# Fetching one half of the transposed tiles between the stores of the other, and holding one batch's channel steps out of four of every six slots

## The chip, the cores and the metric

The kernel runs on one core of a Trainium2 chip. The metric is the device time of one execution in microseconds (us); lower is better. Besides it there is one profiled execution of the kernel before, with a trace of every instruction on the five engines and of the DMA packets.

## The reference

The program is a block-sparse attention followed by a Fourier mixer with a two-layer channel network, for 4 batches, 8 heads, 768 rows and head size 64 (512 columns when the heads stand side by side).

```python
# attention, per batch and head
scores = scale * q @ k.T                      # 768 x 768
scores = where(mask, scores, -1e9)            # mask of 32 x 32 blocks: window, first, last, sampled
attn   = exp(scores - max) / sum
x      = attn @ v                             # heads side by side: (768, 512) per batch
# mixer, per batch
mixed = real(fft(fft(x, axis=rows), axis=columns))
u     = x + mixed
un    = (u - mean(u)) / sqrt(var(u) + 1e-6)   # along the 512 columns
out   = u + relu(un @ w_ch1) @ w_ch2          # 512 -> 2048 -> 512
```

## The kernel before

**Slots.** Attention works on pairs of heads: 4 pairs for a batch, 16 in all. A pair is cut into 6 *slots* of two units each (128 keys by 384 queries, two heads), so there are 96 slots, numbered 0 to 95, and 24 of them make a *phase*, one for each batch. In `slot(sl)`, `phase, r = divmod(sl, SB)` gives the phase and the slot within it (0 to 23), and `n, s = divmod(sl, SP)` the pair and the slot within the *pair* (0 to 5). A slot does scores on TensorE (line 579), the exponential on ScalarE (607), the multiplication by the mask on VectorE (609, from the second batch's end on; before that TensorE adds the mask itself, line 589), the sums along the keys on GpSimd (639, or on VectorE in line 634) and the product with v on TensorE (653). Scores have two PSUM buffers, so a unit's scores wait until the mask multiplication two units earlier has read its buffer.

**The mixer of a batch** runs during the phase of the next batch, in two lists. `apart` holds the small steps, most of them VectorE work: folds, the two Fourier products, mean and variance (`spread`), whitening (`whiten`, kind "w", it waits for GpSimd's 1/sqrt, `rstd_at`), and then for each of two halves of three tiles `un_blocks`: VectorE transposes the whitened tile in 32 x 32 blocks and SyncE (SP) stores it to a scratch tensor in device memory (`far<-un`, line 1016, 256 KB). When all six are stored, `un_back` reads both halves back with the blocks in their transposed places, four DMAs of 192 KB for each half (`unT<-far`, line 1025, runs of 128 bytes). Four steps `right` of kind "b" (line 1057, VectorE) then need both halves. `late` holds the channel network: 4 rounds, each of two *quads* (line 1103, seven products in place of eight) and six *channel* steps (line 1268). If a round's first quad is started while attention stands still (`state["alone"]`), and it isn't the fourth, its second product is done with seven products in place of eight as well (`round_of`, line 1211, three steps in place of six).

**What sets the order.** The order of all instructions is fixed when the program is built, by a planner that keeps a clock of its own for every engine (`when`) and adds a cost written by hand for each step. Steps of `apart` go into gaps of TensorE (`gap`), and, in phases 2 and 3, up to four at the end of a slot while `late` is empty. A "b" step is taken only when the planner's clock has passed `state["back"]`, which `un_back` sets to its own time plus `BACK[b]`. Channel steps go into the odd slots by an allowance, `owed`: each slot adds `pace`, the planned time of `late` above `COVER` = 100 us divided by the slots left, between 2.5 and 9.6 us, and a step is taken while `owed` is at least half its cost (9.1 us a quad, 3.45 us a channel step; a whole batch is 155.6 us). In slot 4 of the first pair of phases 2 and 3, `until(..., s == 4)` takes all channel steps of the batch before last that are left, alone, until its first half is stored; the rest of the second half follows in the next slots.

**The SP queue** issues its DMAs in the order of the program: besides the two kinds above, the loads of q, k and v (`qb` line 231, `kb` line 231, `vr` line 271), the stores of the output (line 1279) and, for later pairs, the exchange of the attention's output through device memory, `row<-oT` (line 692) and `x<-row` (696). The tile `oT` has one buffer: VectorE's transpose into it (line 661) waits until the last `row<-oT` has read it.

Of the kernel before, what the change touches and what calls it, by code (L numbers as in the profile page):

```python
# [11 lines left out]
FP32 = mybir.dt.float32  # L12
# [10 lines left out]
def _words(ap, n):  # L23

    return bass.DRamTensorHandle(ap.tensor.name, (2 * n,), I32)
# [74 lines left out]
def kernel(  # L100
# [14 lines left out]
    nc = tc.nc  # L115
# [4 lines left out]
    P = 128  # L120
    C = S // P
    BLK = 32
# [5 lines left out]
    ND = DM // P  # L128
    NF = FF // P
    T = C // 2  # L130
# [51 lines left out]
    tr_p = ctx.enter_context(tc.tile_pool(name="tr_p", bufs=2))  # L182
# [11 lines left out]
    when = {"PE": 0.0, "ACT": 0.0, "DVE": 0.0, "POOL": 0.0}  # L194
    free = {"m": [0.0, 0.0], "t": [0.0]}

    def busy(engine, us, after=0.0):
        when[engine] = max(when[engine], after) + us
        return when[engine]
# [11 lines left out]
    HOP = 0.1  # L211
# [89 lines left out]
    def bit(n):  # L301
# [5 lines left out]
                      in_=bass.AP(tensor=_words(sampled_blocks, NB * NR), offset=0,  # L307
                                  ap=[[0, NB], [1, 2 * NB * NR]]))
# [183 lines left out]
    s_at, e_at, e_free, oT_at, acc_at = {}, {}, {}, {}, {}  # L492
# [100 lines left out]
    def weigh(u, s):  # L593
        n, w = divmod(u, UP)
        half, c = divmod(w, C)
        e = ep.tile([P, 2, HS], FP32, tag="e", name="e")
        e_of[u] = e
        if u in by_pe:
            nc.scalar.activation(out=e, in_=s[:, :, 0:HS], func=ACT.Exp, scale=scale)  # L599
            e_at[u] = busy("ACT", 0.8, max(s_at[u], e_free.pop(u - 2 * SLOT, 0.0))) + HOP  # L600
            if n >= NP:
                to_gather.append(u)

            if w >= UP - SLOT:
                gather_to(u)
        else:
            nc.scalar.activation(out=s[:, :, 0:HS], in_=s[:, :, 0:HS], func=ACT.Exp, scale=scale)  # L607
            m = mask[:, c, half * HS:(half + 1) * HS].rearrange("p (o s) -> p o s", o=1)
            nc.vector.tensor_tensor(out=e, in0=s[:, :, 0:HS], in1=m.broadcast_to([P, 2, HS]),  # L609
                                    op=ALU.mult)  # L610
            e_at[u] = busy("DVE", 0.97, busy("ACT", 0.8, s_at[u]) + HOP) + HOP
            gather_to(u)
            if n >= NP:
                gather(u)

    def gather_to(u):
        while to_gather and to_gather[0] <= u:
            gather(to_gather.popleft())

    def gather(u):  # L620


        n, w = divmod(u, UP)
        half, c = divmod(w, C)
        if c == 0:
            return
        if c == 1:
            acc_of[n, half] = acc_p.tile([P, 2, HS], FP32, tag="acc", name="acc")
        acc, e = acc_of[n, half], e_of[u]
        start = e_of[u - 1] if c == 1 else acc  # L630
        at = max(e_at[u], acc_at.get((n, half), 0.0))
        sooner = max(when["DVE"], at) + 1.0 < max(when["POOL"], at) + 2.9
        if u in by_pe and masks["by_pe"] and w < UP - SLOT and sooner:
            nc.vector.tensor_tensor(out=acc, in0=start, in1=e, op=ALU.add)
            acc_at[n, half] = busy("DVE", 1.0, at) + HOP
        else:

            for i in range(2):
                nc.gpsimd.tensor_add(out=acc[:, i, :], in0=start[:, i, :], in1=e[:, i, :])  # L639
            acc_at[n, half] = busy("POOL", 2.9, at) + HOP  # L640
        e_free[u] = acc_at[n, half]

    def values(u):
# [335 lines left out]
    rstd_at = deque()  # L979
# [3 lines left out]
    def mixer(b, xA, xB):  # L983


        uns, unT = {}, {}
# [21 lines left out]
        lines = {}  # L1008

        def un_blocks(half, m):  # L1010

            un = uns.pop((half, m))
            if half not in lines:
                lines[half] = far_p.tile([T, P, DM], FP32, tag=f"un{half}", name="far")
            nc.vector.transpose(out=un, in_=un)
            nc.sync.dma_start(out=lines[half][m], in_=un)

        def un_back():

            for half in range(2):  # L1020
                unT[half] = tr_p.tile([P, ND, T * P], FP32, tag="tr", name="unT")
                of = lines[half].rearrange("m (g j) (k a i) -> a j k (m g) i",
                                           j=BLK, a=P // BLK, i=BLK)
                for a in range(P // BLK):
                    nc.sync.dma_start(
                        out=unT[half][BLK * a:BLK * a + BLK].rearrange(
                            "j k (g i) -> j k g i", i=BLK),
                        in_=of[a])
            state["back"] = max(when["PE"], state["ready"]) + BACK[b]

        t, s = {}, {}
        K1, K2 = slice(0, ND // 2), slice(ND // 2, ND)
# [289 lines left out]
        def outputs(r, m, after):  # L1322
# [60 lines left out]
            if r == 1:  # L1383
# [5 lines left out]
              for h in range(2)]  # L1389

        ft = [[("d", lambda h=h, m=m: un_blocks(h, m), 0.0, 0.0, 0.7) for m in range(T)]
              for h in range(2)]

# [23 lines left out]
        for r in range(0 if last else NF // 4):  # L1417
# [9 lines left out]
    MOST, LEAST = 9.6, 2.5  # L1427
    COVER = 100.0
    AHEAD = 2.2
    BACK = 13.0, 12.0, 15.0  # L1430
    ALONE = 3.0
    LEAVES = 13.0
    SP = UP // SLOT
# [2 lines left out]
    short, apart, late, due = deque(), deque(), deque(), deque()  # L1436
    asked = set()
    needed = set()
    state = {"paired": False, "total": None, "w": 0, "got": 0, "owed": 0.0, "ready": 0.0,
             "back": 0.0, "place": None,  # L1440
             "alone": False, "drain": lambda: None}
# [10 lines left out]
    def do_apart():  # L1452
        kind, fn, pe, act, dve, _ = apart.popleft()
        if finished and kind[0] in "mt" and state["total"] in short:
            short.remove(state["total"])
            state["total"][2]()
        if kind[0] in "dwb":
            dve += behind(kind)
            state["ready"] = busy("DVE", dve, {"w": rstd_at[0] if rstd_at else 0.0,
                                               "b": state["back"]}.get(kind, state["ready"])) + HOP  # L1460
            fn()
            return
        done = state["ready"]
        if kind != "-":
            at = bank(kind[0])
            done = busy("PE", pe, done) + HOP
        fn()
        if act:
            done = busy("ACT", act, done) + HOP
        if dve:  # L1470
            done = busy("DVE", dve, done) + HOP
        if kind != "-":
            give(at, done - HOP)
        state["ready"] = done
# [44 lines left out]
    def begin(b):  # L1519


        before, after, rest = mixer(b, x_of[b, 0], x_of[b, 1])
        any_of = len(late) + len(apart) + 4 * len(rest)
        hold = 2 * T
        apart.extend((*step, any_of) for step in norm_steps(b) + before)
        apart.extend((*step, hold) for step in after)

        def go():
            late.extend(rest)
        apart.append(("-", go, 0.0, 0.0, 0.0, hold))  # L1530
# [21 lines left out]
    def slot(sl):  # L1552
        phase, r = divmod(sl, SB)
        n, s = divmod(sl, SP)
# [56 lines left out]
        if s >= ((4 if late else 5) if reuse else 3) and (n, 0) in oT_at and once(n):  # L1611
            b, j = pairs[n]
            at = oT_at[n, 0]
# [12 lines left out]
        if sl < B * SB and n % NP == 1 and s == 1:  # L1626
            b = pairs[n - 1][0]
            at = oT_at[n - 1, 1]
            if b >= 2:
                until(lambda: (b - 2, 1) in finished)  # L1630
                at = when["PE"] + LEAVES
# [22 lines left out]
        us = sum(step[1] for step in late)  # L1654
        pace = max(LEAST, min(MOST, (us - COVER) / left)) if left > 0 else MOST
        state["owed"] = min(state["owed"], pace) + pace if late else 0.0
        more = paired and opens and sl < B * SB
        if not more:
            gap(rest())
# [3 lines left out]
            gap(rest())  # L1663

        for _ in range(4 if phase > 1 and not late and len(apart) < 6 * T else 0):
            if apart and not late and (apart[0][0] != "b" or
                                       state["back"] < max(when["DVE"], when["PE"]) + 0.2):
                do_apart()


# [6 lines left out]
        while short and (not more or soon) and (  # L1677
                s in must or len(short) > 1 or phase == 0 or soon or sl == B * SB):
            ready = [i for i in short if max(i[1], min(free[i[0]])) <= when["PE"] + 0.1]
# [36 lines left out]
    for sl in range(B * SB + 1):  # L1716
        slot(sl)
        if sl == B * SB - 4:
            flag = highest()
        if sl == B * SB - 2:  # L1720
            over = nc.values_load(flag[0:1, 0:1], min_val=0, max_val=1)
# [7 lines left out]
    def general():  # L1729
# [4 lines left out]
        for b in range(B):  # L1734
            xs = [xp.tile([P, T, DM], FP32, tag=tag, name="x") for tag in ("xA", "xB")]
            for h in range(H):
# [43 lines left out]
                for half, x in enumerate(xs):  # L1780
                    sl = slice(half * T, half * T + T)
                    nc.vector.tensor_tensor(out=x[:, :, h * D:(h + 1) * D], in0=op[:, sl, :],
                                            in1=rs[:, sl, :].broadcast_to([P, T, D]),
                                            op=ALU.mult)
            before, after, rest = mixer(b, *xs)
            for step in before + after:
                step[1]()
# [42 lines left out]
```

## Time and profile before

| | us |
|---|---|
| median of 3 runs | 1061.82 (1060.11 to 1062.27) |
| the profiled execution | 1062.32 |
| its span, first to last instruction | 1060.2 |
| TensorE busy | 1014.9 (96% of the span) |
| VectorE busy | 712.8 (67%) |
| ScalarE busy | 373.2 (35%) |
| GpSimd busy | 327.3 (31%) |
| mean granted TensorE clock | 0.986 |

TensorE carries the kernel: the chain that ended last lies on it for 82% of the span. The trace has one start of scores for each slot: slot 24 starts at 123.5 us, slot 48 at 225.2, slot 72 at 533.3; the last, slot 95, at 768.3, and what follows is the mixer of the last two batches. In the profile, "SPq" is the SP queue's DMA issue (start and length of the issue, not of the transfer), a number in square brackets is the idle time of that engine just before the row and what ended it, and the tables by window give the share of the full TensorE clock that was granted ("PEclk").

### The profile page before, as it was taken

The page shows a single profiled execution, that of the slowest core. Times are in us where ns is not written, and L with a number is a line of the kernel's source. Part 1 is how long each engine was busy: PE and PEld are TensorE (multiplying, and loading weights), DVE is VectorE, ACT ScalarE, POOL GpSimd, SP SyncE. Part 2 cuts the span into 40 slices and gives each one's busy share as a digit, 9 for nine tenths or more (in the row PEclk, how much of TensorE's full clock was granted, in tenths as well). Part 3 has the DMA queues.
Part 4 walks back from the last instruction along what each step waited for, and adds up shares of the span by engine and source line. Part 5 has one row for each costly group of instructions (what it writes and reads, how often), then busy time and mean ns, then how long its engine had stood idle before and what let it go on. Part 6 is the DMA issues. An engine that isn't in the chain of part 4 may idle for free.

```text
span 1060.2 us, 13059 instructions
## 1 busy us (share of the span) xinstructions
PE 1014.9 (96%) x4526; PEld 564.1 (53%) x4526; DVE 712.8 (67%) x1292; ACT 373.2 (35%) x763; POOL 327.3 (31%) x363
## 2 busy tenths in 40 slices
PE   8999999999999999799999999869999999999996
PEld 4333345435776853344544764334454764578575
DVE  6898795969776567574579477656357575674663
ACT  6978755563122223343241223333120221210210
POOL 1000183565733306373354222743340221000000
PEclk9999999999999999899999999989999999999998
DMA  7857522292000014732120002731000001000001
GB/s 213 233 168 220 113 46 45 50 141 35 1 1 1 1 46 115 104 64 46 30 45 1 1 11 72 137 65 23 11 18 10 1 1 41 19 1 1 0 17 47
DMA packets 163461, 58.12 MB, mean 55 GB/s; under 512 B 144172, under 2 KB 154170, under 8 KB 163386
## 3 DMA queue, kind: packets, MB, share of 16 engines
q1 hardware_dynamic: 162134, 56.45, 23.9%
q8 instruction: 38, 0.62, 0.3%
q10 hardware_dynamic: 1220, 0.72, 0.3%
q14 instruction: 37, 0.30, 0.1%
q0 software_dynamic: 32, 0.01, 0.0%
HBM read 43.80 MB, written 13.37 MB: 54 GB/s over the span
## 4 chain that ended last, share of the span: by engine, by line
PE 82%; DVE 7%; ACT 3%; POOL 2%; DMA 2%; issue 2%; SPq 2%; DVEq 0%; ACTq 0%; POOLq 0%
PE z L1103 16%; PE y L1268 12%; PE s L579 10%; PE o L653 8%; PE yp L1103 8%; PE yy L1336 7%; PE xp L1103 4%; PE yz L1211 3%; PE yw L1211 2%; PE yc L1211 2%; PE zp L861 2%; DVE e L609 1%; POOL acc L639 1%; PE s L589 1%; ACT e L599 1%
## 5 line engine op out<-in xcount | busy, mean ns | idle before, releaser
L639 POOL TENSOR_TENSOR acc<-acc,e 128x384 f32<-128x384 f32 x162 | 165.8, 1056 | 84.8 <-DVE e L609 62.2
L579 PE MATMUL s<-qT,kT 64*128 64x384 f32 x768 | 157.6, 525 | 28.8 <-DVE e L609 22.3
L653 PE MATMUL o<-e,vr 128*64 128x384 f32 x768 | 143.0, 499 | 0.0
L579 PEld LDWEIGHTS s<-qT,kT 64*128 64x128 f32 x768 | 64.7, 188 | 112.2 <-DVE e L609 42.7
L607 ACT ACTIVATE s<-s 128x768 f32<-128x768 f32 x86 | 65.7, 793 | 133.2 <-PE s L579 125.7
L639 POOL TENSOR_TENSOR acc<-e 128x384 f32<-128x384 f32 x40 | 44.7, 1137 | 212.7 <-ACT e L599 125.2
L609 DVE TENSOR_TENSOR e<-s,mask 128x768 f32<-128x768 f32 x86 | 78.3, 948 | 36.7 <-ACT s L607 31.1
L599 ACT ACTIVATE e<-s 128x768 f32<-128x768 f32 x106 | 80.9, 811 | 53.3 <-PE s L589 34.9
L1103 PE MATMUL z<-unT,t 128*128 128x384 f32 x256 | 93.3, 487 | 0.8 <-DVE hA L1108 0.8
L653 PEld LDWEIGHTS o<-e,vr 128*64 128x64 f32 x768 | 48.0, 137 | 71.0 <-issue 68.6
L1108 DVE TENSOR_TENSOR hA<-z,hA 128x384 f32<-128x384 f32 x64 | 35.6, 556 | 67.0 <-PE z L1103 66.9
L1112 ACT ACTIVATE hA<-hA 128x384 f32<-128x384 f32 x64 | 33.5, 523 | 123.4 <-DVE hA L1108 123.4
L1268 PE MATMUL y<-w_sb,hB 128*128 128x512 f32 x168 | 75.2, 596 | 0.0
L1268 PE MATMUL y<-w_sb,hA 128*128 128x512 f32 x168 | 75.1, 595 | 0.0
L1224 POOL TENSOR_TENSOR x<-of,x 128x256 f32<-128x256 f32 x45 | 34.8, 780 | 125.2 <-ACT of L1216 85.2
L1103 PEld LDWEIGHTS z<-unT,t 128*128 128x128 f32 x256 | 48.4, 190 | 35.6 <-DVE hA L1108 2.4
L1271 DVE TENSOR_TENSOR x<-y,x 128x512 f32<-128x512 f32 x42 | 28.9, 688 | 54.8 <-PE y L1268 54.8
L1112 ACT ACTIVATE hB<-hB 128x384 f32<-128x384 f32 x64 | 33.5, 523 | 86.3 <-DVE hB L1108 86.3
L1268 PEld LDWEIGHTS y<-w_sb,hB 128*128 128x128 f32 x168 | 31.1, 190 | 38.8 <-issue 38.6
L1268 PEld LDWEIGHTS y<-w_sb,hA 128*128 128x128 f32 x168 | 31.1, 190 | 37.3 <-issue 36.0
L1103 PE MATMUL xp<-unT,w_sb 128*128 128x384 f32 x128 | 49.9, 515 | 0.0
L1103 PE MATMUL yp<-unT,w_sb 128*128 128x384 f32 x128 | 47.4, 493 | 0.0
(236 smaller groups left out, 1703.8 us busy)
## 6 DMA issues: line engine op xcount, KB each, us to landing
wraw<-in_moe_w_ch_dram SPq DMA_DIRECT2D x32, 512.0 KB
vr<-in_v_dram SPq DMA_DIRECT2D x30, 192.0 KB
far<-un SPq DMA_DIRECT2D x18, 256.0 KB
unT<-far SPq DMA_DIRECT2D x24, 192.0 KB
qb<-in_q_dram SPq DMA_DIRECT2D x44, 96.0 KB
kb<-in_k_dram SPq DMA_DIRECT2D x44, 96.0 KB
out_dram<-x SPq DMA_DIRECT2D x11, 252.0 KB
out_dram<-x SPq DMA_DIRECT2D x18, 128.0 KB
```

Of the source, the lines that this page charges most:

```text
L579: nc.tensor.matmul(s[:, i, 0:HS], kT[rows, c * P:(c + 1) * P], qT[rows, queries], start=True, stop=u not in by_pe)
L599: nc.scalar.activation(out=e, in_=s[:, :, 0:HS], func=ACT.Exp, scale=scale)
L607: nc.scalar.activation(out=s[:, :, 0:HS], in_=s[:, :, 0:HS], func=ACT.Exp, scale=scale)
L609: nc.vector.tensor_tensor(out=e, in0=s[:, :, 0:HS], in1=m.broadcast_to([P, 2, HS]), op=ALU.mult)
L639: nc.gpsimd.tensor_add(out=acc[:, i, :], in0=start[:, i, :], in1=e[:, i, :])
L653: nc.tensor.matmul(o[D * i:D * i + D, :], vt[:, i, c, :], e[:, i, :], start=(c == 0), stop=(c == C - 1))
L1103: nc.tensor.matmul(to, a[:, k, :], c[:, k, :], start=(k == 0), stop=(k == ND // 2 - 1))
L1108: tt(out=to, in0=ps, in1=a, op=ALU.add)
L1112: nc.scalar.activation(out=h, in_=h, func=ACT.Relu)
L1211: nc.tensor.matmul(to, a[:, k, :], c[:, k, :], start=start and k == 0, stop=k == 1, skip_group_check=True)
L1268: nc.tensor.matmul(y, hs[0, half][:, l, m * P:(m + 1) * P], w2_sb[:, 4 * r + l, :], start=(l == 0), stop=(l == 3))
L1336: nc.tensor.matmul(ps, a[:, k, :], c[k // 2][:, k % 2, :] if isinstance(c, list) else c[:, k, :], start=(k == 0), stop=(k == 3))
```

## The change

Four things change in the planner's program; no arithmetic does.

1. The planner's cost of one unit's sum on GpSimd goes from 2.9 to 2.4 us, where it chooses between VectorE and GpSimd and where it advances GpSimd's clock.
2. `un_back` is split in `fetch(0)` and `fetch(1)`. `fetch(0)`, the first half's four DMAs, is issued right after the first store of the second half, if fewer than six channel steps are left; `un_back` issues what is not yet issued. `BACK` becomes 12, 12, 14, with 5 us more if the first half wasn't fetched early.
3. In phase 2, in the slots with `s < 4`, the allowance for channel steps is set to zero. (`s` counts the slot within the pair, so this is four of every six slots of the phase.)
4. In the loop at the end of a slot, a "w" step is now put off, as a "b" step is, until the planner's clock has passed the time at which its 1/sqrt is due.

```diff
-        sooner = max(when["DVE"], at) + 1.0 < max(when["POOL"], at) + 2.9
+        sooner = max(when["DVE"], at) + 1.0 < max(when["POOL"], at) + 2.4
...
-            acc_at[n, half] = busy("POOL", 2.9, at) + HOP
+            acc_at[n, half] = busy("POOL", 2.4, at) + HOP
...
             nc.sync.dma_start(out=lines[half][m], in_=un)
+            if half == 1 and len(late) < 2 * T:
+                fetch(0)
+
+        def fetch(half):
+
+            if half in unT:
+                return
+            unT[half] = tr_p.tile([P, ND, T * P], FP32, tag="tr", name="unT")
+            of = lines[half].rearrange("m (g j) (k a i) -> a j k (m g) i",
+                                       j=BLK, a=P // BLK, i=BLK)
+            for a in range(P // BLK):
+                nc.sync.dma_start(
+                    out=unT[half][BLK * a:BLK * a + BLK].rearrange(
+                        "j k (g i) -> j k g i", i=BLK),
+                    in_=of[a])
 
         def un_back():
 
-            for half in range(2):
-                unT[half] = tr_p.tile([P, ND, T * P], FP32, tag="tr", name="unT")
...
-            state["back"] = max(when["PE"], state["ready"]) + BACK[b]
+            late_by = 0.0 if 0 in unT else HALF
+            fetch(0)
+            fetch(1)
+            state["back"] = max(when["PE"], state["ready"]) + BACK[b] + late_by
...
-    BACK = 13.0, 12.0, 15.0
+    BACK = 12.0, 12.0, 14.0
+    HALF = 5.0
...
         state["owed"] = min(state["owed"], pace) + pace if late else 0.0
+        if phase == 2 and s < 4:
+            state["owed"] = 0.0
...
         for _ in range(4 if phase > 1 and not late and len(apart) < 6 * T else 0):
-            if apart and not late and (apart[0][0] != "b" or
-                                       state["back"] < max(when["DVE"], when["PE"]) + 0.2):
+            if apart and not late and (
+                    {"b": state["back"], "w": rstd_at[0] if rstd_at else 0.0}.get(apart[0][0], 0.0)
+                    < max(when["DVE"], when["PE"]) + 0.2):
                 do_apart()
```

More of the change, by code (lines that the diff above doesn't have):

```diff
@@ L1016, in un_blocks @@
             nc.sync.dma_start(out=lines[half][m], in_=un)
-        def un_back():
-            for half in range(2):
-                unT[half] = tr_p.tile([P, ND, T * P], FP32, tag="tr", name="unT")
[L1022 to L1028, printed above, removed]
-            state["back"] = max(when["PE"], state["ready"]) + BACK[b]
+            if half == 1 and len(late) < 2 * T:
[11 more added lines that the diff above has]
+                    in_=of[a])
+        def un_back():
+            late_by = 0.0 if 0 in unT else HALF
+            fetch(0)
+            fetch(1)
+            state["back"] = max(when["PE"], state["ready"]) + BACK[b] + late_by
         t, s = {}, {}
```

## The prediction

> **What bounds the kernel now.** I read the granted clock and spans first (one core, 0.986), then the page: PE is busy for 1014.9 of 1060.2 us, and of the 40 slices only three in the middle show an 8 or less, two of them with a lower clock. So I looked for the places where PE stands still. The timeline has two large ones, at the same point of phases 2 and 3. The first (slots 60 and 61):
>
> ```profile
> 429.48 1.78 PE L579 MATMUL s<-qT,kT 64*128 64x384 f32 x8 [1.29 <-DVE e L609]
> ...
> 435.54 0.96 DVE L1057 TENSOR_TENSOR t<-unT 128x768 f32<-128x768 f32 x1 [5.26 <-DMA unT<-far]
> ...
> 440.15 2.93 PE L579 MATMUL s<-qT,kT 64*128 64x384 f32 x8 [6.17 <-DVE e L609]
> ```
>
> VectorE waits 5.26 us for the tiles to come back; the mask multiplications stand behind its four "b" steps, and PE waits 6.17 us for those. In phase 3 (slots 85, 86):
>
> ```profile
> 673.69 11.10 SPq L1025 DMA_DIRECT2D unT<-far  x8
> ...
> 688.53 2.74 SPq L692 DMA_DIRECT2D row<-oT  x4
> ...
> 692.86 0.58 DVE L661 STREAM_TRANSPOSE oT<-o 128x384 f32<-128x384 f32 x1 [5.57 <-DMA row<-oT]
> ...
> 697.93 2.29 PE L579 MATMUL s<-qT,kT 64*128 64x384 f32 x6 [8.40 <-DVE e L609]
> ```
>
> Here the tiles are back in time, but `row<-oT` stood on the SP queue behind all eight fetches, and VectorE waits 5.57 us for it before its "b" steps. In both places the clock falls after the standstill, as the windows show (last but two column):
>
> ```profile
> 444.00:446.00 2.00, 2.00 (x5) 1.09 (x4) 1.84 (x2) 0.03 (x1) 0.00 (x0) 0.50 0.86 134
> ...
> 698.00:700.00 2.00, 2.00 (x6) 1.06 (x8) 2.00 (x3) 0.37 (x1) 1.98 (x3) 0.50 0.88 140
> ```
>
> At half clock the scores of slot 61 take 2.93 us, those of slot 59 at full clock 1.72, other slots 1.56. The first five products of the quad behind them (20 matmuls, 443.01 to 451.28) take 8.27 us, elsewhere 6.72. So the first standstill costs 1.37 + 1.55 = 2.9 us beyond its idle time; the second, by its scores (2.93) and its values (3.47 for 2.80), 2.0 us.
>
> In phase 1 there is no such place. There VectorE also waits for the tiles (until 238.31), but the chain of waits from 226 to 246 us is PE work from end to end: TensorE adds the masks, so nothing waits for VectorE.
>
> **The early fetch, first batch:** nothing on the path, 0, for the reason just given (its cover is PE's attention work; were it gone, VectorE's 3.8 us wait would show).
>
> **The early fetch, second batch (gain A).** Eight fetches take from 420.49 (first issue) to 435.54 (VectorE starts): 15.05 us, 1.88 each. With four issued earlier, the other four need 7.5 us from their own issue. When can that be? The SP queue around it:
>
> ```profile
> 402.71 0.33 SPq L1016 DMA_DIRECT2D far<-un  x1
> 403.29 1.51 SPq L1279 DMA_DIRECT2D out_dram<-x  x3
> 404.90 6.83 SPq L231 DMA_DIRECT2D kb<-in_k_dram  x4
> 411.85 1.62 SPq L1279 DMA_DIRECT2D out_dram<-x  x3
> 413.58 0.35 SPq L1016 DMA_DIRECT2D far<-un  x1
> ```
>
> The moved four go in at 403.04. Behind them stand these rows and then three more stores of the output (414.76), two loads of v (416.60) and the last tile store (420.12). The moved issues take 4.25 us (phase 1, 223.90 to 228.15) to 5.45 (420.49 to 425.94), perhaps 1.5 more where the k loads, already slow at 1.7 us each, meet a fuller queue. SP has idle time to give back: 0.7 us before 414.76 and 2.15 before 420.12. So the last tile store moves 1.4 to 4.1 us back, to 421.5–424.2. One wait is new. Today the four fetches right behind that store read the other half; in the changed order they read what it has just written. The trace's packets of the store issued at 402.71 end at 404.35, 1.65 us later. The second four thus start at 423.2–425.9 and are back at 430.7–433.4; VectorE comes to them at 430.3. A gains 2.1 to 4.8 us of the 5.26; I take the middle, 3.5. [...]
>
> The loads of k are needed at 427.13 and land with some 10 us to spare. The output stores may matter: ScalarE's copy into that tile at 422.44 must wait for them, and they move by 3 to 5 us; up to 2 us of ScalarE, part of the range.
>
> The standstill of PE falls from 6.17 to about 2.7 us. Does the clock still fall? In phase 0 a gap of 2.38 us brought it down:
>
> ```profile
> 70.00:72.00 2.00, 1.92 (x8) 0.96 (x10) 1.90 (x4) 2.00 (x6) 0.00 (x0) 0.68 0.78 199
> 72.00:74.00 2.00, 2.00 (x11) 0.82 (x9) 1.93 (x5) 2.00 (x5) 0.00 (x0) 0.50 1.01 370
> ```
>
> while gaps of 1.68 (before 419.90) did not. So half of the 2.9 us, or all; I take 2.0. [...]
>
> **The early fetch, third batch (gain B).** The same shift puts the last tile store of 673.32 to 674.7–677.4; 1.65 us later four fetches of 5.65 us (679.14 to 684.79) end at 682.0–684.7 in place of 684.79. `row<-oT`, and ScalarE's wait for `qb`, move up by 0.1 to 2.8 us. I take 1.5, and 0.3 of clock (PE still stands for 7 us). `BACK` 14 leaves the order: counted from `un_back`, the planner's clock stands at +13.1 at the end of slot 83, and passes 14 in slot 84, as it passed 15. Bounds: 0 and the whole 5.57 + 2.0.
>
> **The allowance at zero.** In the first pair of phase 2 `late` is empty until slot 52 and all of it runs alone: three rounds with line 1211 (263 to 282, 301 to 320, 340 to 363) are there before. If `late` fills a slot earlier, the zero keeps the first quad out of slot 51: no change. The second batch's `late` fills in slot 61. Today slots 61, 65, 67, 69 and 71 take four quads and six channel steps, so round 1's first quad is not alone. Changed: 61, 63, 67 and 69 take none; slot 64 adds (155.6 − 100)/9 = 6.2, slot 65 adds 6.95, and 13.1 pays one quad (4.0 is left, below half a quad); slots 70 and 71 add 9.6 each and pay a quad and three channel steps; 73 and 75 one channel step each. One channel step of round 0 is left at slot 76, and rounds 1 and 2 begin alone, where today only round 2 does. One more round in the short form: three steps take 18.8 us (263.23 to 282.00), six channel steps 20.9 (twice 10.46): 2.0 us gained, 1.2 if the waits of round 1 in batch 0 (0.78 and 0.41) come too. The other PE work is moved, not added.
>
> It costs cover: slots 61 to 64 and 66 to 70 run without channel work. Slots 62 to 64 do so today with no gap of PE:
>
> ```profile
> 459.07 1.56 PE L579 MATMUL s<-qT,kT 64*128 64x384 f32 x8
> 460.56 1.51 PE L653 MATMUL o<-e,vr 128*64 128x384 f32 x8
> 462.00 1.72 PE L579 MATMUL s<-qT,kT 64*128 64x384 f32 x8
> ```
>
> slots 56 to 60, with more VectorE work, with 1.68 + 1.29 us, 0.6 a slot. So 0 to 5.4 us for nine slots; I take 1.3, near the first, whose VectorE load is the same.
>
> **The other two edits.** Line 639 measures 1.0 to 1.1 us, two for a unit, so 2.4 is nearer than 2.9. Choices change only until the first channel step (243 us), where PE stands for some 3 us in 120: 0, bounds 1 us either way. The wait for "w": with 2.4 the planner has the 1/sqrt due at 419.2, before VectorE's planned 420.0, so the step isn't put off and the real 2.65 us wait (DVE 414.73 to 417.38) stays: 0; if it is put off, up to 1.7 us gained in each of two phases.
>
> **The sum.** A 3.5 + 2.0, B 1.5 + 0.3, round 2.0, less 1.3: 8.0 us. From the profiled 1062.32 that is 1054.3; the median is 0.5 below the profiled run, so **1053.8**. Measurement can tell about 0.2% (2.1 us) from no change.
>
> **Rivals.**
> - *Both standstills go entirely* (SP hides the moved issues): 5.26 + 2.9 + 5.57 + 2.0 + 2.0 − 1.3 = 16.4, 1045.4. For it: four fewer fetches ahead of `row<-oT`; against: SP has only 2.9 us of idle time. 15%.
> - *The transfer ends no sooner*: SP loses at 403 and at the store what it saves later. A = B = 0: 0.7 gained, 1061.1. 12%.
> - *It does not add a short round*: if a second quad slips into slot 71, 1055.8. 5%.
> - *Slower: the held slots starve.* Without channel work each of the nine slots idles as slot 56 did, 1.68 us, because a mask stands behind other VectorE work: 15.1 in place of 1.3, 1067.6. It outweighs the 9.3 gained from 1.04 us a slot on. For it: slots 56 to 60; against: 62 to 64. 18%.
>
> The forecast has 50%, its own range 1049 to 1059. The range of 8 in 10 runs from 1046 to 1063.5. Faster 0.73 (the forecast, the first and third rival and a little of the second), within 0.2% 0.07, slower 0.20.
>
> **What would show it.** Four `unT<-far` between the first two second-half stores; the wait before line 1057 near 436 us down to 0–3 and no 0.50 window as long as 6.8 us; `row<-oT` of 688.5 a little earlier; no line 1103 in slots 61 to 64; two rounds of line 1211 in phase 3's time alone, where there was one. Wrong: new PE gaps between 440 and 515 us of over 1 us a slot, or a wait before 1057 as long as today.

## The result: slower by 1.0%

The changed kernel takes 1071.72 us (median of 4 runs, 1071.49 to 1072.95) against 1061.31 us before (4 runs): a ratio of 1.0101, 95% interval 1.0084 to 1.0119, some 10.4 us more. The forecast was 1053.8 us, faster. Its profiled execution has a span of 1070.2 us (before 1060.2).

The page of the changed kernel (its span, PE's row, and the group of the short rounds' additions, which had 45 before):

```profile
span 1070.2 us, 13212 instructions
PE 1018.8 (95%) x4562; PEld 570.8 (53%) x4562; DVE 720.6 (67%) x1302; ACT 377.5 (35%) x772; POOL 346.5 (32%) x386
L1233 POOL TENSOR_TENSOR x<-of,x 128x256 f32<-128x256 f32 x54 | 41.9, 782 | 128.0 <-ACT of L1225 75.7
```

The last line has 54 additions instead of 45, so one more round runs in the short form, as intended. PE is busy 3.9 us longer and idle 39.5 us instead of 33.0 up to its last matmul.

Where the time went is read from the start of the scores of each slot, after minus before: −0.3 us at slot 24, +2.6 at slot 49, **+10.4 at slot 50, +14.8 at slot 52, +14.1 at slots 53 to 56**; +13.2 at slot 77, +11.9 from slot 88, and +10.0 at the end. So the first batch costs 14 us, 2.9 of them ahead of slot 49, and phases 2 and 3 and the rest give back 4. The prediction had put the first batch at 0.

First, the two places that the prediction was about. The timeline of the changed kernel, phase 2 (four rows) and phase 3 (one):

```profile
434.68 2.52 PE L579 MATMUL s<-qT,kT 64*128 64x384 f32 x8 [2.35 <-DVE e L609]
441.52 3.94 SPq L1028 DMA_DIRECT2D unT<-far  x4
450.17 1.77 DVE L1066 TENSOR_TENSOR t<-unT 128x768 f32<-128x768 f32 x1 [2.93 <-DMA unT<-far]
455.59 2.56 PE L579 MATMUL s<-qT,kT 64*128 64x384 f32 x8 [4.65 <-DVE e L609]
...
707.28 2.93 PE L579 MATMUL s<-qT,kT 64*128 64x384 f32 x8 [4.38 <-DVE e L609]
```

VectorE's wait for the tiles falls from 5.26 to 2.93 us, PE's from 6.17 to 4.65 and from 8.40 to 4.38. But ahead of them a wait grew from 1.68 to 2.35 us, in both phases, and the windows (last but two column) show that this one brings the clock down by itself, before the second does again:

```profile
436.00:438.00 2.00, 2.00 (x9) 0.60 (x7) 0.96 (x1) 1.20 (x2) 2.00 (x3) 0.50 0.78 167
456.00:458.00 2.00, 2.00 (x8) 0.55 (x4) 1.08 (x3) 0.80 (x1) 0.00 (x0) 0.50 0.18 50
```

The half-clock stretch of 6.8 us at 439 before is now two of 3.4 us, at 435.5 and 456.0, and the one of 10.2 us at 691.9 is now one of 3.4 us (688.1) and one of 6.8 us (705.2): nothing of the clock came back in either phase.

Now the first batch. The SP queue there, and who waits, in the changed kernel:

```profile
216.34 5.37 SPq L1028 DMA_DIRECT2D unT<-far  x4
221.75 1.64 SPq L1016 DMA_DIRECT2D far<-un  x2
226.12 4.16 SPq L1028 DMA_DIRECT2D unT<-far  x4
230.39 3.26 SPq L231 DMA_DIRECT2D qb<-in_q_dram  x4
...
237.08 0.84 ACT L536 ACTIVATE qT<-qb 128x768 f32<-128x768 f32 x1 [6.05 <-DMA qb<-in_q_dram]
...
238.44 0.90 PE L676 MATMUL xt<-ident,oT 128*128 128x128 f32 x3 [5.54 <-ACT oT L664]
```

and the same stretch of the queue before:

```profile
218.97 2.18 SPq L231 DMA_DIRECT2D qb<-in_q_dram  x4
...
223.90 10.00 SPq L1025 DMA_DIRECT2D unT<-far  x8
```

The load of the queries of pair 9 stood *ahead* of the last tile store and of all eight fetches; it now stands *behind* them, 11.4 us later. ScalarE, which runs its steps in the order of the program, stands at the squares of these queries (line 536) for 6.05 us; behind them stands the copy of `oT` (664) that PE's transpose (676) waits for. PE idles 5.54 us, and then the clock is at half for 6.8 us (237.6 to 244.4). A second wait follows, for sums that VectorE does only after a "b" step:

```profile
248.70 1.75 DVE L1066 TENSOR_TENSOR t<-unT,t 128x768 f32<-128x768 f32 x1
250.97 0.72 PE L751 MATMUL st<-ident,sums 128*128 128x128 f32 x3 [1.93 <-DVE sums L708]
```

No edit of the change names that load. In the planner's order `un_back` now comes in slot 45, ahead of the call that loads pair 9; before it came in slot 46, behind it.

### The profile page after: what moved, and what is told of

The parts are those of the page before. It is cut to its first block, busy times and chain, and to the rows that moved or that the text cites. A ratio compares the mean times of both kernels' runs of the same rounds, so it can differ in the third digit from the quotient of the medians.

```text
span 1070.2 us, 13212 instructions
## 1 busy us (share of the span) xinstructions
PE 1018.8 (95%) x4562; PEld 570.8 (53%) x4562; DVE 720.6 (67%) x1302; ACT 377.5 (35%) x772; POOL 346.5 (32%) x386
## 4 chain that ended last, share of the span: by engine, by line
PE 76%; DVE 11%; ACT 3%; DMA 3%; issue 3%; POOL 1%; SPq 1%; DVEq 0%; ACTq 0%; POOLq 0%
PE z L1112 15%; PE y L1277 10%; PE s L579 8%; PE yp L1112 7%; PE o L653 7%; PE yy L1345 6%; PE yz L1220 4%; PE xp L1112 4%; PE yw L1220 3%; PE yc L1220 3%; PE zp L861 2%; DVE t L1066 1%; DVE e L609 1%; DMA unT<-far 1%; PE sp L724 1%
## 5 line engine op out<-in xcount | busy, mean ns | idle before, releaser
L639 POOL TENSOR_TENSOR acc<-acc,e 128x384 f32<-128x384 f32 x166 | 169.1, 1055 | 73.8 <-DVE e L609 42.9
L653 PE MATMUL o<-e,vr 128*64 128x384 f32 x768 | 146.0, 508 | 0.0
L1233 POOL TENSOR_TENSOR x<-of,x 128x256 f32<-128x256 f32 x54 | 41.9, 782 | 128.0 <-ACT of L1225 75.7
L1277 PE MATMUL y<-w_sb,hB 128*128 128x512 f32 x144 | 65.0, 597 | 0.0
L1277 PE MATMUL y<-w_sb,hA 128*128 128x512 f32 x144 | 63.8, 594 | 0.0
L1280 DVE TENSOR_TENSOR x<-y,x 128x512 f32<-128x512 f32 x36 | 24.8, 688 | 49.5 <-PE y L1277 49.5
L1112 PE MATMUL xp<-unT,w_sb 128*128 128x384 f32 x128 | 47.5, 494 | 0.0
L1112 PE MATMUL z<-t,w_sb 128*128 128x384 f32 x128 | 46.6, 487 | 0.2 <-DVE t L1066 0.2
L1112 PE MATMUL z<-t,t 128*128 128x384 f32 x128 | 46.5, 486 | 0.0
```

What stands on the lines that cost most here:

```text
L653: nc.tensor.matmul(o[D * i:D * i + D, :], vt[:, i, c, :], e[:, i, :], start=(c == 0), stop=(c == C - 1))
L1112: nc.tensor.matmul(to, a[:, k, :], c[:, k, :], start=(k == 0), stop=(k == ND // 2 - 1))
L1233: nc.gpsimd.tensor_add(out=to, in0=kept[i], in1=to)
L1277: nc.tensor.matmul(y, hs[0, half][:, l, m * P:(m + 1) * P], w2_sb[:, 4 * r + l, :], start=(l == 0), stop=(l == 3))
```

## The experiments

**Which edit moved the load?** Theory 1: the sum step's 2.4. Theory 2: the early fetch. Four kernels. *The 2.4 put back:*

```diff
-  max(when["POOL"], at) + 2.4   ...   busy("POOL", 2.4, at)
+  max(when["POOL"], at) + 2.9   ...   busy("POOL", 2.9, at)
```

> The changed kernel with one number put back: the planner's cost of a sum step on GpSimd is 2.9 again, not 2.4; all else stays changed (early fetch, guard, put-off of w, new BACK). In the plan the load of the queries of pair 9 then stands ahead of the first batch's last tile store and second fetch, as it did before the change. Theory 1 (the 2.4 shifted the plan by a slot and put that query load behind the fetch, 237.08 squares waiting 6.05 us for qb, about 14 us lost in the first batch): the slots from 50 on no longer start 10 to 14 us late, PE's 5.54 us wait at 238.4 and the two stretches at half clock behind it are gone, and the time is 1057 to 1060 us. Theory 2 (fetching the first batch's first half early is what disturbs SyncE's queue there): the time stays near 1071 us and PE still waits about 5 us near 238.

Measured 1067.22 us (1.0054, 1.0037 to 1.0070). The first batch is whole again: slot 53 starts 1.5 us after that of before, of which 1.0 dates from slot 13. PE's wait near 238 us is gone. But phases 2 and 3 now lose 2.6 and 3.3 us (below); that part was not expected by theory 1.

*The 2.4 alone, on the kernel before:*

```diff
-  2.9   (both places)
+  2.4
```

> The kernel before with one edit alone: GpSimd's sum step is put down at 2.4 instead of 2.9. No early fetch, no guard, no put-off. In its plan the fetch of both halves of the first batch, eight transfers, again stands ahead of the query load of pair 9. Theory 1: slower by 8 to 14 us (1069 to 1075 us), with squares of pair 9 waiting for qb and PE waiting 4 to 7 us between 230 and 245 us of the span. Theory 2: within 2 us of before (1060 to 1063 us).

1079.70 us (1.0174, 1.0157 to 1.0191), more than either theory said; slot 53 is 14.6 us late without any early fetch, since the load of q (232.48) again stands behind the eight fetches (222.38 to 232.38):

```profile
240.82 0.90 PE L676 MATMUL xt<-ident,oT 128*128 128x128 f32 x3 [6.96 <-ACT oT L664]
...
425.83 0.48 ACT L677 COPY x<-xt 128x384 f32<-128x384 f32 x1 [13.88 <-DMA out_dram<-x]
428.88 2.93 PE L579 MATMUL s<-qT,kT 64*128 64x384 f32 x8 [13.37 <-DVE e L609]
```

The last two rows are a second mechanism, met again below: line 677 copies into a new x tile, whose two buffers are free only when an older batch's output stores have landed. This kernel also does one short round fewer than before (36 additions of that line instead of 45).

*The first batch not fetched early, the rest as changed:*

```diff
-            if half == 1 and len(late) < 2 * T:
+            if half == 1 and b > 0 and len(late) < 2 * T:
...
-    BACK = 12.0, 12.0, 14.0
-    HALF = 5.0
+    BACK = 13.0, 12.0, 14.0
+    HALF = 0.0
```

> The changed kernel, the 2.4 kept, but the first batch's first half is not fetched early (both halves come together, with BACK 13, 12, 14); the second and third batches as changed. The query load of pair 9 stays behind the fetch in the plan. Theory 1: no recovery, 1069 to 1075 us, since all eight transfers now stand ahead of it. Theory 2: the first batch's loss goes, 1056 to 1060 us.

1072.54 us (1.0107): no recovery, as theory 1 said; slot 53 is 14.4 us late. The early fetch is not what hurts the first batch.

*The changed kernel, with that load a slot earlier:*

```diff
-        if s >= (4 if paired else 3) and n + 2 < len(pairs) and ...
+        if s >= (4 if paired else 2 if n == 7 else 3) and n + 2 < len(pairs) and ...
```

> The changed kernel whole, with one load moved: the query load of pair 9 is issued a slot earlier, in slot 44, ahead of the first batch's last two tile stores and its second fetch; the plan is otherwise the changed one. Theory 1: qb lands before squares want it, PE's 5.54 us wait near 238 goes, and 9 to 14 us come back: 1058 to 1063 us. If part of the loss lies in the whitening steps that the 2.4 moved ahead of slot 50's sums (PE waits 1.93 us for L751 at 251, and the clock halves behind it), 3 to 5 us of it stay and the time is 1062 to 1066 us. Theory 2 (the early fetch disturbs the queue): above 1066 us.

1064.88 us (1.0035, 1.0020 to 1.0049): 6.8 of the 10.4 us come back by moving one load, and ScalarE's wait for it is gone. At slot 53 7.9 us are left, of which 2.9 arise between slots 24 and 49, and 4.9 between slots 51 and 52, at the second wait: four "b" steps (237.56 to 244.2) stand before the sums.

```profile
244.73 0.55 PE L751 MATMUL st<-ident,sums 128*128 128x128 f32 x3 [3.27 <-DVE sums L708]
```

So the first batch's loss is the 2.4: by the place of the load on SP, and by the "b" steps' place on VectorE (this second part is read from the trace; no run moved those steps alone). The 2.9 us ahead of slot 49 are there in all four kernels with the 2.4, and not with the 2.9 put back; 1.8 of them are a wait of PE for sums on VectorE that the kernel before doesn't have (line 706, before 160.28 in the changed kernel). Theory 2 falls for this batch.

**What are the other three edits worth?** The first run left phases 2 and 3 slower than expected, so theory 3 puts a loss on the early fetch itself. All three kernels keep 2.9. *Fetch and guard, without the put-off of "w":*

```diff
 (the changed kernel with 2.9, and)
-            if apart and not late and ({"b": state["back"], "w": ...}.get(...) < ...):
+            if apart and not late and (apart[0][0] != "b" or state["back"] < ...):
```

> The changed kernel without its two edits of the planner's rules: GpSimd's sum step at 2.9 again, and the steps named w not put off. Early fetch, guard and the new BACK stay. The plan then orders loads and fetches of the first batch as before, and un_back of the second and third batches comes in the slot where it came before the change. In the run with 2.9 alone put back, slots 54 to 77 lost 2.6 us and slots 77 to the end 3.3 us, where the changed kernel gained 0.9 and 1.3; PE waited 4.28 and 4.19 us for the mask multiplication at 427 and 683 us. Theory 1 (both planner edits harm through the order that they make, the fetch and the guard help): these two waits shrink to 1.7 to 2.4 us, first batch within 1 us of before, and the time is 1055 to 1059 us. Theory 3 (the early fetch itself pushes other loads back, whatever the order): 1060 to 1064 us.

1063.00 us (1.0012, 1.0003 to 1.0020), in theory 3's range. Slots 59 and 60 lose 3.6 us, slots 83 to 85 3.8.

*The early fetch alone:*

```diff
 (the kernel before, with fetch(0) after the first store of the second half)
```

> The kernel before with the early fetch alone: no guard, no change of the planner's rules, the old BACK values. Theory 1: PE's waits of 6.17 and 8.40 us for the whitening fall to 4 to 5 us each as in the changed kernel (4.65 and 4.38), nothing else moves, 1056 to 1059 us. Theory 3: what the fetch gains is lost to loads behind it, 1060 to 1063 us.

1064.98 us (1.0031, 1.0021 to 1.0041), above both ranges: the early fetch by itself makes the kernel slower. PE's long waits did fall (6.17 to 5.11, 8.40 to 6.52), but slots 57 to 60 lose 3.0 us ahead of the first. The timeline there:

```profile
419.18 2.15 SPq L1288 DMA_DIRECT2D out_dram<-x  x3
425.35 0.33 SPq L1016 DMA_DIRECT2D far<-un  x1
427.56 0.48 ACT L677 COPY x<-xt 128x384 f32<-128x384 f32 x1 [4.06 <-DMA far<-un]
428.96 3.97 SPq L1028 DMA_DIRECT2D unT<-far  x4
```

and before:

```profile
414.76 1.75 SPq L1279 DMA_DIRECT2D out_dram<-x  x3
420.12 0.33 SPq L1016 DMA_DIRECT2D far<-un  x1
422.44 0.49 ACT L677 COPY x<-xt 128x384 f32<-128x384 f32 x1
```

The bracket names the tile store, issued 2.2 us before; the chain of waits, which follows the semaphores back, has an output store that lands at 427.33, just ahead of the copy:

```profile
419.80 7.54 DMA out_dram<-x
```

The four early fetches push the output stores back by 4.4 us; ScalarE's copy into the new x tile waits for them (4.06 us where there was no wait), and so do the exps behind it. The last tile store, too, is issued 5.2 us later, after SP has waited 2.5 us for the output stores. The second four fetches thus begin at 428.96, where before the second four began at 426.04.

*The guard alone:*

```diff
 (the kernel before, and)
+        if phase == 2 and s < 4:
+            state["owed"] = 0.0
```

> The kernel before with the guard alone: no channel step in the third batch's first four slots. By the sum of the prediction one more short round saves 2.0 us of PE and keeping the slots bare costs up to 1.3: 1059 to 1061 us, with 9 more GpSimd additions of the round line than before (45 to 54). If the bare slots leave PE without cover, PE waits 2 us or more between slots 62 and 72 and the time is 1063 us or more.

1059.10 us (0.9978, 0.9970 to 0.9987): **faster than both kernels**, by 2.4 us. It has 54 additions of line 1224 instead of 45; slots 61 to 77 gain 1.7 us, and nowhere between slots 62 and 72 does PE wait as long as 1 us.

**Why does the tile store land so late?** In the changed kernel's chain of waits the last tile store is the longest piece around 440 us:

```profile
435.25 6.21 DMA far<-un
```

*Fetch and guard, the second half's output stores issued by ScalarE:*

```diff
-                store(half, m)
+                store(half, m, queue=nc.scalar if half == 1 else nc.sync)
```

> As the kernel with fetch and guard alone, and the output stores of a batch's second half are issued by ScalarE instead of SyncE. In the changed kernel the second and third batches' last tile store lands 6.21 us after its issue, and SyncE stands waiting for it. If the output stores ahead of it on SyncE's queue are the cause, it lands within 2 to 3 us, the whitening begins 3 to 4 us sooner in each of two batches, and the time is 3 to 7 us below the run of fetch and guard. If the stores use the same DMA engines at the same time whoever issues them, or ScalarE loses time in issuing and waiting, no gain or a loss of up to 4 us against that run.

1065.10 us (1.0040), no gain: 2.1 us more than fetch and guard. The store still needs 4.09 us (426.30 to the next fetch at 430.39), with no output store ahead of it on its queue and the last of ScalarE's issued by 420.80: output stores ahead of it on the queue are not the only cause. The semaphore times in the traces before and after the change show more. There the last tile store of the second and third batches lands 0.48 to 0.64 us after the transfer issued just ahead of it, whatever that is: in the kernel before a load of v (423.82, the store 424.35; 677.14, the store 677.62), in the changed kernel an output store (440.83, the store 441.46; 692.92, the store 693.56). The store of 402.71 in the kernel before, with nothing still moving ahead of it, landed in 2.0 us. So in these four cases the store landed late together with what was issued ahead of it; why those transfers take so long stays open. PE waits 3.73 us at 404, where ScalarE stands 5.0 us ahead of its exps around the store that it issues.

*The fetch behind the stores, ahead of the last tile store:*

```diff
+            if half == 1 and m == 0 and len(late) < 2 * T:
+                fetch(0)
             nc.vector.transpose(out=un, in_=un)
             nc.sync.dma_start(out=lines[half][m], in_=un)
-            if half == 1 and len(late) < 2 * T:
-                fetch(0)
```

> As the kernel with fetch and guard, but the first half's four transfers are put on SyncE's queue directly ahead of the last tile store, that is behind the output stores, k and v loads that the changed kernel puts them ahead of. In the kernels with the early fetch ScalarE stood 4.1 to 4.6 us at the copy into a new x tile until the output stores of the first batch had landed (out_dram<-x issued at 419.99, landed 7.48 us later). Theory 4 (the four transfers delay these output stores, and the new x tile waits for them): ScalarE's wait at that copy goes back to under 1.6 us, slots 58 to 60 and 83 to 85 lose no 3 us any more, and the time is 1056 to 1060 us, at or below the guard alone (1059.1). Rival (the early fetch loses because the second fetch stands bare behind the last tile store's landing, wherever the first one goes): 1061 to 1064 us, with SyncE still waiting 2.5 us or more between the last tile store and the second fetch.

1065.84 us (1.0039): a miss for theory 4 in the time. Its mechanism is seen: ScalarE waits for no output store at line 677, and slots 59, 60 and 83 to 85 lose nothing. But the rival's mechanism wins, with a time above its range too:

```profile
427.83 1.39 SPq L1018 DMA_DIRECT2D far<-un  x1
431.68 4.18 SPq L1028 DMA_DIRECT2D unT<-far  x4
```

(Line 1018 is the tile store in this kernel.) The four fetches (422.14, 5.59 us) now delay the last tile store, SP stands 3.85 us from its issue to the next, with nothing else to issue, and VectorE gets the tiles at 440.07, 4.5 us later than before the change.

*The guard alone, un_back fetching the second half first:*

```diff
-            for half in range(2):
+            for half in (1, 0):
```

> As the kernel with the guard alone, but un_back fetches the second half first and then the first half. Before the change the first half's four transfers go out while the last tile store is landing; here the second half's come directly behind that store, so that SyncE must stand for the whole landing. This measures the landing in the surroundings of the kernel before. If it takes 3.4 to 6.2 us as in the kernels with the early fetch, SyncE waits that long in each of three batches, the whitening begins 3 to 6 us later in two of them, and the time is 1064 to 1070 us against 1059.1 with the guard alone. If it takes 1.65 us as the prediction assumed: 1060 to 1063 us.

1064.52 us (1.0031), against 1059.10 for the guard alone: 5.4 us for an uncovered landing. This measures it:

```profile
422.07 0.33 SPq L1016 DMA_DIRECT2D far<-un  x1
425.76 10.45 SPq L1025 DMA_DIRECT2D unT<-far  x8
```

3.69 us from issue to the next issue. In the kernel before, the first half's four issues (5.45 us) filled just this time: the store of 420.12 lands at 424.35, and they last until 425.94. That is what the early fetch took away.

*"w" put off, alone, on the kernel before* (the last edit of the change, nothing else):

```diff
-            if apart and not late and (apart[0][0] != "b" or state["back"] < ...):
+            if apart and not late and ({"b": state["back"], "w": ...}.get(...) < ...):
```

> The kernel before with one edit alone: the steps named w are put off until 1/std is due, with GpSimd's sum step still at 2.9. With fetch and guard this edit cost 1067.2 against 1063.0 us. Theory 1 (it moves un_back and what hangs on it a slot later in two batches, whatever else is there): 1063 to 1067 us. Rival (it harms only together with the early fetch): 1060 to 1062 us.

1062.15 us (1.0004, 0.9994 to 1.0014): no difference; the rival holds. With fetch and guard it cost 4.2 us (1067.22 against 1063.00); by which wait was not followed up. With the 2.4 the planner's order is the same with and without it, so in the changed kernel it does nothing.

*The early fetch issued by ScalarE:*

```diff
-                fetch(0)
+                fetch(0, nc.scalar)      # its four dma_start go to that queue
```

> As the kernel with fetch and guard, but the first half's four early transfers are issued by ScalarE, so that they stand ahead of nothing on SyncE. Theory 5 (the early fetch loses by its place on SyncE: it pushes the output stores back by the 5 us of its four issues, and the last tile store and the copy into the new x tile wait for these stores): the stores go out near 411.9 to 416.5 of the span as before the change, the last tile store near 420, and only its landing (3.69 us with the swap) stands bare: the whitening's wait falls by 0 to 3 us a batch and the time is 1055 to 1060 us, at or below the guard alone (1059.1). Rival (the transfers use the same DMA engines whoever issues them, or ScalarE's four issues hold up exps): 1061 to 1066 us, with PE waiting 2 us or more for the mask multiplication between 403 and 411.

1091.74 us (1.0272, 1.0258 to 1.0286), far outside both. ScalarE is held by the four issues, whose last waits for output stores to land, and the exps stand behind it:

```profile
414.43 11.52 ACTq L1028 DMA_DIRECT2D unT<-far  x4
426.06 1.50 ACT L607 ACTIVATE s<-s 128x768 f32<-128x768 f32 x2 [12.37 <-DMA out_dram<-x]
427.90 2.93 PE L579 MATMUL s<-qT,kT 64*128 64x384 f32 x8 [11.12 <-DVE e L609]
```

Theory 5 is not shown by this: PE's later waits are down to 4.07 and 5.48 us (guard alone: 6.29 and 8.65), but at another offset of all engines, so that only the price of the issuing engine is clear.

## Why the prediction was wrong, step by step

- **"The other two edits … 0, bounds 1 us either way": this step failed, and it decided the sign.** It costed the 2.4 by its choices between VectorE and GpSimd. But the number also advances the planner's clock, and by that `un_back` came a slot earlier, ahead of the load of pair 9. Its bound for the choices failed as well: 2.9 us went between slots 24 and 49. Measured 8.7 us (all edits, 1071.72, less fetch and guard, 1063.00); alone 18.8. That "w" would not be put off was right, and its 2.65 us wait (DVE 431.49) stays.
- **"The early fetch, first batch: 0"** holds for the fetch (not fetching it early gave 1072.54), but the premise, that VectorE's wait is covered, looked at the wrong waiter. What stood behind the fetch on SP, q of pair 9, had no cover: ScalarE 6.05 us, PE 5.54.
- **Gain A (3.5 + 2.0) and gain B (1.5 + 0.3).** The step that failed is the landing of the last tile store. The prediction took 1.65 us, from the packets of another store; it is 3.7 us by the swap and up to 6.2 in the changed kernel. In the kernel before, the store of 420.12 lands at 424.35 and the second four fetches start at 426.04: at most 1.7 us were to be had, before any delay. The last tile store moved 5.2 us with the fetch alone, where 1.4 to 4.1 were expected: the 2.15 us that SP was to give back before 420.12 are no slack but a wait for the output store issued at 412.28 to land (420.06). With the fetch alone the wait for an output store stays (2.5 us, until the tile store goes out at 425.35).
- **"The output stores may matter … up to 2 us of ScalarE, part of the range"** named the right wait and undersized it: 4.06 us of ScalarE, 3.0 of PE. Instead of 7.3 us gained by A and B, the fetch alone loses 3.3 (ratio 1.0031).
- **The clock.** Half the 2.9 us or all of it was to come back; none did, since the wait of 2.35 us brought 3.4 us at half clock and the one of 4.65 us another 3.4. But the prediction's reading, that the length of a wait decides, does not hold: a wait of 1.69 us was followed by slow scores with the fetch alone (2.40 us from 420.26, and the values 2.12 for 1.51), one of 1.68 us was not in the kernel before (scores 1.78 us), and neither was one of 2.62 us with the fetch alone (scores 1.78 us from 684.84). In the kernel before, the half-clock stretches up to PE's last matmul start whole steps of 3.41 us apart (70.71, 439.35, 691.94 and 903.57, that is 108, 74 and 62 steps) and last one to three steps (3.41 to 10.24 us); in the changed kernel they start whole steps apart as well. Counted over these two traces, up to PE's last matmul, a step at full clock in which PE was busy for 0.37 of the time or less was followed by half clock in all nine cases, one with 0.50 or more in none; of the three between, the one at 0.43 was not and those at 0.44 and 0.45 were. By this count it matters how much of a wait falls into one step.
- **The allowance at zero** was right in its mechanism: no quad in slots 61 to 64, rounds 1 and 2 of the second batch alone, 54 additions. Its size was off to the good side: 0.7 net foreseen, 2.4 measured alone (1.4 to 3.2); the cover that it was charged for (1.3) costs hardly anything. Not all of it is shown to be the guard's: between the two profiled executions 1.7 us are gained in slots 61 to 77, 0.6 lost again by slot 88, and 1.8 gained behind the last slot, where the kernel before has 3.4 us at half clock from 903.6, behind waits of PE of 1.16 and 0.73 us; that the guard takes this stretch away was not shown. The rival that the held slots starve is refuted: PE's one gap of over 0.5 us in slots 62 to 72 is 0.53.
- Of the rivals, "the transfer ends no sooner" came nearest for the fetch, but had it at no loss. The slower rival rested on another mechanism than the one that came.

By medians: guard −2.4, early fetch on top of it +3.9, the 2.4 on top of both +8.7, "w" 0: +10.2, of the +10.4 measured. These are steps from one kernel to the next, so they must add up; what an edit costs depends on the others, since the 2.4 alone costs 18.8.

## What to carry to other kernels

In a program whose order comes from a planner, a changed cost is a changed order: before pricing it by the step that it belongs to, list which DMA issues change places, and who waits for each. A transfer moved forward on an in-order queue is paid by all that it now stands ahead of (with the fetch alone, output stores issued 4.4 us later); ask of each of those who needs its landing, tile buffers to be freed included. And before moving work out of a place, ask what that work hides there: here it hid a store's landing (3.69 us by the swap).

## What was not expected of the hardware

- In phases 2 and 3 the last 256 KB tile store took 3.7 (the swap) to 6.2 us (the changed kernel) until a transfer that reads it could be issued, though another such store, with nothing moving ahead of it, landed in 2.0 us and its packets ended after 1.65.
- SP, and ScalarE when it issues, waited for output stores to land before issuing an unrelated transfer: 2.1 us before 420.12 in the kernel before, 2.5 us with the fetch alone, and part of the 12.37 us above. The traces show what they waited for. In the kernel before, the 414 transfers that SP and ScalarE issue carry eight semaphores, 51 or 52 each, and take them in turn: 394 of 406 times a semaphore is taken again by the eighth issue after. Ahead of 350 of those 406 issues the trace has a wait for that same semaphore. SP's wait ahead of the store of 420.12, which ends at 420.09, is one of them: the output store of 412.28 had the semaphore last, and its last update came at 420.06. In the kernel whose fetch ScalarE issues, the last fetch (issued at 425.39) waited for an output store of 417.09 that landed at 425.37. SP's waits in the kernel before, from 400 to 445 us (line, what it waited for, us in all, times, longest), have the 2.1 us:

```profile
SPq L1016 <- DMA out_dram<-x: 2.1, 1, 2.1
```

- An idle gap of 1.93 us (before 250.97) was followed by 3.4 us at half clock (251.2 to 254.6): it lay whole in one of the steps of 3.41 us, in which PE was busy for 0.44. The gap of 1.68 us before 419.90, in the kernel before, was spread over two steps (0.65 and 1.03 us, PE busy for 0.81 and 0.70) and had no half clock behind it.
